# Two SBUF stacks, expert 0's W1 split inside attention, and a reordered last routing quarter

## The chip, the cores and the metric

One core of one Trainium2 chip runs the whole program. The metric is the device time of one execution in microseconds (us); less is better. PE is TensorE, DVE VectorE, ACT ScalarE, POOL GpSimd, and SP the queue of SyncE, which issues transfers.

## The reference: what is computed

The reference chains three layers, all in float32. Clustered attention: queries and keys are given to the nearest of 16 centroids, and a query sees only the keys of its cluster. A mixture of 8 experts: each token goes to its best expert (at most 384 tokens per expert, in token order), weighted by the softmax of the gate. A gated layer (SwiGLU) over all tokens.

```python
mask = q_assign[:, :, :, None] == k_assign[:, :, None, :]
attn = softmax(where(mask, scale * q @ k.T, -1e9))         # 2 batches, 8 heads, 768 x 768
x = (attn @ v) laid out as 1536 tokens x 512
logits = x @ w_gate; e = argmax(logits); gate_w = softmax(logits)[e]
y = relu(x @ w1[e]) @ w2[e]        # tokens of expert e, 512 -> 1024 -> 512
x = gate_w * y
out = (silu(x @ w_gate2) * (x @ w_val)) @ w_out            # 512 -> 1536 -> 512
```

## The kernel before

Attention (`Attention`, lines 24 to 534) works through 16 heads in 8 pairs. A head has 6 tiles of 128 queries, so its loop `run` (L430) has 96 steps g, called slots here. A slot writes out, by the token order in `CFG["order"]`, what each engine does: the exponential of the next tile's scores (token S, `soft`, ACT, L352), every third slot the evacuation of a finished product (E, `evac`, ACT L398 and DVE L400), the scores two tiles ahead (Q, `qk`, PE L339, with the row maximum nm on DVE, L342), the transposes of the tile's probabilities P in two halves (T0 and T1, `pt`, PE L368; ACT copies the first half to SBUF in L371, DVE the second in L373), background work (B0, B1: preparing the next pair), `onat` (O) and every third slot the product with V (V0, `pv`, L387). Each half of the transposes takes a PSUM tile with the tag t from a pool of two buffers (`ps_t`). The scores use two buffers s. Every engine executes its own list in order.

`onat` (L404) turns a finished half of a pair's output into token rows x and adds its part of the gate's logits lg: a matmul with the matrix R (identity and gate weights), and two DVE products with the reciprocal row sums rs (L421).

When the last pair of a batch has a half done, that quarter of the tokens is routed by the generator `Router.route` (L613). It gives control back after every operation, and `trickle` in `run` takes one step of it per slot (token B1), from slot 84 on two (tokens T0 and S). It sums the logits over heads (rlo), takes the maximum, the one-hot roh of the first best expert, the gate weight rgw = 1 / (sum of exponentials + 1e-9), ranks (four small matmuls into another tile t of `ps_t`, L650 to L653, read by DVE in L654), slots in the expert's list (rslot), and then scales each of three tiles of x by rgw (ACT, L666) and scatters it to rows in DRAM (`scatter`, POOL, L602, after a memset of one word named gap). In this generator the rank matmuls and their reader L654 are emitted in the same step.

Behind the loop `run` (L521 to L534) issues the last product, finishes the third quarter's generator, some transposes of the identity that keep PE busy (`warm`), `evac`, `onat`, and the fourth quarter's generator to its end. Then the experts start (`Experts.run`, L936): the read xr of expert 0's rows waits for all scatters, POOL clears Y, four chunks of W1 are split into a high part (ACT cast, L813) and a low part (DVE subtraction, L814), PE runs fillers (L949, L952, L960), DVE computes the offsets of the experts (offi), and expert 0's rows are transposed (`xt`, L841) and split into X, on which the first expert matmul (L879) waits. W2's chunks are split on ACT and POOL inside the expert. `NRAW` = 4 raw buffers hold chunks on their way from DRAM; splitting a chunk issues the read of the one four places on.

All SBUF pools of attention (`at1` to `at3`, and x and lg) are closed together when attention ends; W1, W2 and Y are allocated in their place after that.

Of the kernel before, what the change touches and what calls it, by code (L numbers as in the profile page):

```python
# [23 lines left out]
class Attention:  # L24


    def __init__(self, tc, ctx, q, k, v, cent, gate, x, lg, ident, raw):
# [7 lines left out]
        self.x, self.lg, self.ident, self.raw = x, lg, ident, raw  # L35
        H, S, D, C, E, J = self.H, self.S, self.D, self.C, self.E, self.J
        self.NP = self.B * H // 2
        one = ctx.enter_context(tc.tile_pool(name="at1", bufs=1))
        self.p2 = ctx.enter_context(tc.tile_pool(name="at2", bufs=2))
        self.p3 = ctx.enter_context(tc.tile_pool(name="at3", bufs=3))  # L40
        self.one = one
        self.ps_s = ctx.enter_context(tc.tile_pool(name="ps_s", bufs=2, space=PSUM))
# [3 lines left out]
        self.qB = [one.tile([128, 2, S], F32R, name=f"qB{i}") for i in range(2)]  # L46
        self.kB = [one.tile([128, 2, S], F32R, name=f"kB{i}") for i in range(2)]
        self.R = one.tile([128, H // 2, 2 * D + 2 * E], F32, name="R")
# [21 lines left out]
    def centroids(self):  # L70
# [3 lines left out]
        sq = one.tile([H * C, D], F32, tag="ol", name="sq")  # L74
# [35 lines left out]
    def load(self, n, names="qkv"):  # L110
# [3 lines left out]
        for nm in names:  # L114
            src = getattr(self, nm)
            shape = [128, 2, self.J, self.D] if nm == "v" else [128, self.J, 2, self.D]
            t = self.p2.tile(shape, F32, tag="ld" + nm, name="ld" + nm)
# [15 lines left out]
    def parts(self, n, nm):  # L133
# [5 lines left out]
        st["A" + nm] = self.p2.tile([128, 2, self.S], F32R, tag="A" + nm, name="A" + nm)  # L139
# [182 lines left out]
    def qk(self, g):  # L322
# [4 lines left out]
        if i == 0:  # L327
            if r == 0:
                st["sum"] = self.p3.tile([128, self.J, 2], F32, name="sum")
                st["O"] = self.p2.tile([128, self.S], F32, name="O")  # L330
            self.heads[hd] = dict(P={}, S={}, T={})
# [9 lines left out]
        nm = self.p3.tile([128, 1], F32, name="nm")  # L341
# [3 lines left out]
    def soft(self, g):  # L345
# [5 lines left out]
        P = self.p3.tile([128, 2, HS], F32, name="P")  # L351
# [3 lines left out]
    def pt(self, g, a):  # L355
# [6 lines left out]
        if c == 0 and a == 0:  # L362
            hs["T"][G] = self.p2.tile([128, J, HJ * 128], F32, tag="PT", name="PT")
# [26 lines left out]
    def evac(self, G):  # L390
# [6 lines left out]
        ol = self.one.tile([D, HS], F32, tag="ol", name="ol")  # L397
# [6 lines left out]
    def onat(self, n, half):  # L404
# [6 lines left out]
        rs = self.p2.tile([128, HJ, 2], F32, name="rs")  # L411
# [3 lines left out]
        for jj in range(HJ):  # L415
            j = half * HJ + jj
            nc.tensor.matmul(ps[:, jj, :], lhsT=st["O"][:, j * 128:(j + 1) * 128], rhs=self.R[:, hp, :],
                             start=True, stop=True)
        for dst, c, w in ((self.lg[:, b, js, 2 * hp:2 * hp + 2, :], 2 * D, E),
                          (self.x[:, b, js, 2 * hp * D:2 * (hp + 1) * D].rearrange("p j (r d) -> p j r d", r=2), 0, D)):  # L420
# [9 lines left out]
    def run(self, cent, gate, early, fill, after):  # L430
# [39 lines left out]
        for e in range(self.E):  # L470
            bg.setdefault(14 + 4 * e, []).append(lambda e=e: fill(e))
        self.qk(0)
# [47 lines left out]
        G, n = 2 * NH - 1, self.NP - 1  # L520
        self.pv(G)  # L521
        for _, r in chains:
            while next(r) is not None:
                pass
            moves.append(r)
        self.warm(self.ps_s, "s", 14)
        self.evac(G)
        for _ in self.onat(n, 1):
            pass
        for r in moves:  # L530
            for _ in r:
                pass
        for _ in after(n, 1, lambda: self.warm(self.ps_s, "s", 16)):
            pass  # L534
# [5 lines left out]
class Router:  # L540


    def __init__(self, tc, const, x, lg, cap):
# [11 lines left out]
        self.esl = const.tile([128, J // 2, E], F32, name="esl")  # L555
        self.tok = const.tile([128, B * J], F32, name="tok")
        self.dump = const.tile([128, B * J], F32, name="dump")
        self.cnt = const.tile([128, E], F32, name="cnt")
# [584 lines left out]
NRAW = 4  # L1143
# [99 lines left out]
```

## Time and profile before

| | us |
|---|---|
| runs (3) | 772.0, 772.21, 776.75; median 772.21 |
| the profiled execution | 772.64 |
| its span, first to last instruction | 770.9 |
| PE busy in the span | 748.9 (97%) |
| DVE busy | 518.1 (67%) |
| ACT busy | 396.6 (51%) |
| POOL busy | 267.9 (35%) |

The span holds attention (to about 267 us), the passage to the experts (to 288.71 us), the experts (to about 467 us) and the gated layer. "Busy" of PE counts the fillers too. A timeline row gives the start, the duration, the engine, the line, and the tile written and read; in brackets stands how long the engine had been idle before and whose signal ended that.

### The profile page before, as it was taken

The numbers are of one execution on the slowest core, as the hardware profiler recorded it, in microseconds if no ns is written. First come the engines' busy times: TensorE is split into PE (matmuls) and PEld (weight loads), VectorE is DVE, ScalarE is ACT, GpSimd is POOL, SyncE is SP. The second block draws the span as 40 slices with busy tenths as digits, with TensorE's granted clock in tenths as the row PEclk, the third lists the DMA queues.
The fourth block names the chain that finished last, engine by engine and source line by source line (L and its number), as shares of the span: only waits on it lengthen the run. The fifth ranks groups of instructions, "written<-read, shape, count | busy, mean of one in ns | idle before, by whom it ended". The sixth has DMA issues, their size and how long they took to land.

```text
span 770.9 us, 12615 instructions
## 1 busy us (share of the span) xinstructions
PE 748.9 (97%) x4311; PEld 625.8 (81%) x4311; DVE 518.1 (67%) x875; ACT 396.6 (51%) x738; POOL 267.9 (35%) x244
## 2 busy tenths in 40 slices
PE   8999999999999989999999999999999999999996
PEld 7777777777776679989999998788888888888885
DVE  5668778778787754767676645776766766767433
ACT  5777686777786635667666633454222232222110
POOL 6120210211220177444494432444223333233244
PEclk9899999999999999999999999999999999999999
DMA  8837758537343146787877642232112121110012
GB/s 202 215 76 208 199 185 247 122 84 185 69 131 116 43 165 205 253 247 249 262 242 254 207 127 76 89 102 90 56 58 78 55 82 55 56 55 0 1 55 109
DMA packets 93339, 102.35 MB, mean 133 GB/s; under 512 B 30304, under 2 KB 77408, under 8 KB 93248
## 3 DMA queue, kind: packets, MB, share of 16 engines
q1 hardware_dynamic: 88384, 89.33, 40.4%
q0 software_dynamic: 1920, 6.29, 2.1%
q10 hardware_dynamic: 2944, 5.54, 2.1%
q8 instruction: 55, 0.90, 0.5%
q14 instruction: 36, 0.29, 0.1%
HBM read 68.21 MB, written 12.58 MB: 105 GB/s over the span
## 4 chain that ended last, share of the span: by engine, by line
PE 50%; DVE 4%; ACT 4%; issue 3%; DMA 2%; POOL 1%; ACTq 0%; DVEq 0%; SPq 0%; POOLq 0%
PE o L1104 12%; PE v L1084 11%; PE g L1084 11%; PE yp L879 3%; PE hp L879 3%; PE hp L871 2%; PE yp L871 2%; DMA xr<-moe_rows 2%; PE yp L880 2%; PE hp L880 1%; ACT W1h L813 1%; PE xp L841 1%; ACT W2h L813 1%; DVE cb L1062 1%; POOL out L1115 1%
## 5 line engine op out<-in xcount | busy, mean ns | idle before, releaser
L814 POOL TENSOR_TENSOR W2l<-raw,W2h 128x1024 fp32r<-128x1024 f32 x32 | 76.3, 2401 | 73.7 <-ACT W2h L813 64.8
L342 DVE TENSOR_REDUCE nm<-s 128x1 f32<-128x768 f32 x96 | 91.1, 949 | 12.7 <-PE s L339 11.7
L352 ACT ACTIVATE P<-s,nm 128x768 f32<-128x768 f32 x96 | 86.5, 901 | 13.6 <-DVE nm L342 10.7
L368 PE MATMUL t<-ident,P 128*128 128x128 f32 x576 | 81.8, 275 | 0.8 <-ACT PT L371 0.6
L1093 POOL TENSOR_TENSOR ghl<-u,ghh 128x512 fp32r<-128x512 f32 x36 | 50.0, 1388 | 75.4 <-ACT ghh L1092 75.4
L368 PEld LDWEIGHTS t<-ident,P 128*128 128x128 f32 x576 | 69.1, 141 | 7.8 <-DVE PT L373 2.3
L387 PE MATMUL acc<-PT,ldv 128*64 128x384 f32 x384 | 69.7, 495 | 0.0
L879 PE MATMUL yp<-H,W2h 128*128 128x416 f32 (+1 forms) x224 | 65.3, 363 | 1.7 <-DVE hp L893 1.3
L879 PE MATMUL hp<-X,W1h 128*128 128x416 f32 (+1 forms) x224 | 66.2, 366 | 0.2 <-DVE X L848 0.2
L339 PE MATMUL s<-Ak,Aq 128*128 128x384 f32 x192 | 59.6, 392 | 2.7 <-ACT P L352 2.6
L1112 DVE TENSOR_TENSOR acc<-o,acc 128x512 f32<-128x512 f32 x60 | 41.2, 691 | 30.6 <-PE o L1104 30.6
L371 ACT COPY PT<-t 128x384 f32<-128x384 f32 x96 | 45.7, 476 | 30.1 <-PE t L368 29.9
L1090 DVE TENSOR_TENSOR u<-sg,g 128x512 f32<-128x512 f32 x36 | 24.7, 687 | 54.1 <-ACT sg L1089 54.1
L814 DVE TENSOR_TENSOR W1l<-raw,W1h 128x1024 fp32r<-128x1024 f32 x32 | 49.1, 1562 | 14.7 <-ACT W1h L813 14.4
L1092 ACT CAST ghh<-u 128x512 fp32r<-128x512 f32 x36 | 22.4, 622 | 68.0 <-DVE u L1091 68.0
L880 PE MATMUL hp<-X,W1l 128*128 128x208 f32 (+1 forms) x224 | 56.5, 252 | 0.0
L880 PE MATMUL yp<-H,W2l 128*128 128x208 f32 (+1 forms) x224 | 56.0, 250 | 0.0
L373 DVE COPY PT<-t 128x384 f32<-128x384 f32 x96 | 52.3, 545 | 1.2 <-PE t L368 1.2
L339 PE MATMUL s<-kB,qB 80*128 80x384 f32 (+1 forms) x192 | 51.2, 347 | 1.0 <-ACT kB L274 0.7
L339 PEld LDWEIGHTS s<-Ak,Aq 128*128 128x128 f32 x192 | 29.6, 193 | 27.5 <-ACT P L352 20.1
L387 PEld LDWEIGHTS acc<-PT,ldv 128*64 128x64 f32 x384 | 24.9, 136 | 28.8 <-issue 27.9
L1062 DVE SCALAR_TENSOR_TENSOR cb<-raw,cb 128x512 uint32<-128x512 uint32 x36 | 45.4, 1260 | 1.2
(251 smaller groups left out, 1873.5 us busy)
## 6 DMA issues: line engine op xcount, KB each, us to landing
raw<-in_moe_w SPq DMA_DIRECT2D x64, 512.0 KB, 4.7
Ak<-Hk SPq DMA_DIRECT2D x32, 192.0 KB, 3.9
moe_rows<-zero SPq DMA_DIRECT2D x8, 768.0 KB, 5.1
raw<-in_moe_w_gate SPq DMA_DIRECT2D x12, 512.0 KB, 3.5
raw<-in_moe_w_val SPq DMA_DIRECT2D x12, 512.0 KB, 3.5
raw<-in_moe_w_out SPq DMA_DIRECT2D x12, 512.0 KB, 3.6
xr<-moe_rows ACTq DMA_DIRECT2D x7, 768.0 KB, 6.8
ldq<-in_q SPq DMA_DIRECT2D x16, 192.0 KB, 3.6
```

What stands on the lines that cost most here:

```text
L339: nc.tensor.matmul(ps[:, c, 0:HS], lhsT=ql[:, qs], rhs=kr[:, c * HS:(c + 1) * HS], start=a == 0, stop=a == 1)
L342: nc.vector.tensor_reduce(out=nm, in_=ps[:, :, 0:HS], axis=AX.XY, op=ALU.max, negate=True)
L352: nc.scalar.activation(out=P, in_=ps[:, :, 0:HS], func=AF.Exp, bias=nm, accum_out=self.pairs[n]["sum"][:, i, r:r + 1])
L368: nc.tensor.transpose(ps[:, jj, :], P[:, a, jj * 128:(jj + 1) * 128], self.ident)
L373: nc.vector.tensor_copy(PT[:, js, cs], ps)
L387: nc.tensor.matmul(acc[c * D:(c + 1) * D], lhsT=v[:, c * HJ + j], rhs=PT[:, c * HJ + j, :], start=j == 0, stop=j == HJ - 1, tile_position= ...
L814: (nc.vector if i < 4 else nc.gpsimd).tensor_tensor(out=l, in0=t, in1=h.bitcast(F32), op=ALU.subtract)
L879: self.nc.tensor.matmul(out[:, :, 0:w], lhsT=W[0][:, k, cols], rhs=mov[:, :, k, 0:w], start=k == 0, stop=False)
L880: self.nc.tensor.matmul(out[:, 0, 0:w], lhsT=W[1][:, k, cols], rhs=mov[:, 0, k, 0:w], start=False, stop=k == ks - 1)
L1062: v.scalar_tensor_tensor(out=b, in0=Hw, scalar=0xC0000000, in1=b, op0=ALU.bitwise_and, op1=ALU.bitwise_or)
L1084: nc.tensor.matmul(p, lhsT=W[a], rhs=self.Y[b][:, k, ts], start=i == 0, stop=i == 3 * self.KD - 1)
L1104: nc.tensor.matmul(p[t], lhsT=h[a][:, fc, t * 128:(t + 1) * 128], rhs=W[b][:, fc], start=fc == 0 and i == 0, stop=fc == 1 and i == 2)
```

## The change

1. The pools. Attention's SBUF pools stand on two stacks: on the left what only the preparation of pairs needs, on the right, by lifetime, what the scores, then the products and routing need. Three pools `keep` outlive attention. x is four tiles instead of one, lg lies in one tile with the last of them, and the experts' and the last layer's temporaries use the same tiles of `keep`. The left stack is closed in slot 81, and W1 takes its place.
2. Expert 0's W1. In slot 81 the four raw reads are issued. In slots 85 to 92 each slot splits half a chunk (`piece`): an ACT cast of 128 x 512 and a POOL subtraction. Each second one issues the read of a W2 chunk. Behind attention the four casts and DVE subtractions of W1 are gone; the first two W2 chunks are split there, on ACT and DVE, after a memset of gap that follows the last scatter on POOL, and the clearing of Y comes later.
3. The routing. The exponentials are three ACT operations that sum on the way (`accum_out`), and ACT adds 1e-9. One operation (`scalar_tensor_tensor`) makes the first-best mask from the difference. `edump` folds the subtraction of `dump` into one product. DVE has 4 operations fewer per quarter. The rank matmuls come before the operations et and gw, with the running sum last, and their reader after a pause (`yield True`).
4. The end of `run`. The third quarter's ranks, slots and first scatter are issued before `evac`; the fourth quarter's x is scaled by rs on ACT in six pieces of 128 x 64, and DVE goes from the logits straight to their sum. `warm` has 10 transposes instead of 14, the last filler 14 instead of 24, and the read of expert 0's rows is cut into 1 + 2 tiles instead of 2 + 1.

```diff
-    def onat(self, n, half):
+    def onat(self, n, half, act=None):
...
+            if act and w == D:
+                for jj in range(HJ):
+                    for r in range(2):
+                        act.activation(out=x[:, jj, r], in_=ps[:, jj, r * D:(r + 1) * D], func=AF.Copy,
+                                       scale=rs[:, jj, r:r + 1])
+                yield True
+                return
...
         self.pv(G)
-        for _, r in chains:
-            while next(r) is not None:
-                pass
-            moves.append(r)
-        self.warm(self.ps_s, "s", 14)
-        self.evac(G)
-        for _ in self.onat(n, 1):
-            pass
-        for r in moves:
-            for _ in r:
-                pass
-        for _ in after(n, 1, lambda: self.warm(self.ps_s, "s", 16)):
-            pass
+        on = self.onat(n, 1, nc.scalar)
+        for q, k in ((on, 2), (r, 9)):
+            for _ in range(k):
+                next(q)
+        self.warm(self.ps_s, "s", 10)
+        self.evac(G)
+        for _ in r:
+            pass
+        next(on)
+        last = after(n, 1, lambda: self.warm(self.ps_s, "s", 16))
+        next(last)
+        for q in (on, last):
+            for _ in q:
                 pass
```

Ahead of that `self.pv(G)` the third quarter's generator is now run up to its pause:

```diff
+        while next(r) is not True:
+            pass
         self.pv(G)
```

In `route`:

```diff
-        yield v.tensor_tensor(out=t, in0=lo, in1=bc(mx), op=ALU.is_equal)
-        yield v.tensor_tensor(out=t, in0=t, in1=self.desc, op=ALU.mult)
+        yield v.tensor_tensor(out=d, in0=lo, in1=bc(mx), op=ALU.subtract)
+        for j in range(J):
+            nc.scalar.activation(out=lo[:, j], in_=d[:, j], func=AF.Exp, accum_out=se[:, j:j + 1])
+        nc.scalar.activation(out=se, in_=se, func=AF.Identity, bias=self.eps)
+        yield v.scalar_tensor_tensor(out=t, in0=d, scalar=0.0, in1=self.desc, op0=ALU.is_equal, op1=ALU.mult)
         yield v.tensor_reduce(out=m2, in_=t, axis=AX.X, op=ALU.max)
         yield v.tensor_tensor(out=oh, in0=t, in1=bc(m2), op=ALU.is_equal)
-        yield v.tensor_tensor(out=d, in0=lo, in1=bc(mx), op=ALU.subtract)
-        nc.scalar.activation(out=d, in_=d, func=AF.Exp)
-        yield v.tensor_tensor(out=t, in0=oh.bitcast(F32), in1=self.esl, op=ALU.mult)
-        yield v.tensor_reduce(out=et, in_=t, axis=AX.X, op=ALU.add)
-        yield v.tensor_tensor(out=et, in0=et, in1=self.dump[:, us], op=ALU.subtract)
-        yield v.tensor_reduce(out=se, in_=d, axis=AX.X, op=ALU.add)
-        yield v.tensor_scalar(out=se, in0=se, scalar1=1e-9, scalar2=None, op0=ALU.add)
-        yield v.reciprocal(out=gw, in_=se)
...
+        nc.tensor.matmul(flat(pp), lhsT=self.all, rhs=flat(self.sum), start=False, stop=True)
+        yield v.tensor_tensor(out=t, in0=oh.bitcast(F32), in1=self.edump[:, us], op=ALU.mult)
+        yield v.tensor_reduce(out=et, in_=t, axis=AX.X, op=ALU.add)
+        yield v.reciprocal(out=gw, in_=se)
+        yield True
         yield v.tensor_tensor(out=t, in0=pp, in1=oh.bitcast(F32), op=ALU.mult)
```

In `Experts` and the outermost function:

```diff
+    def piece(self, i, k):
...
+        self.nc.scalar.copy(out=h[:, ks], in_=t[:, ks])
+        self.nc.gpsimd.tensor_tensor(out=l[:, ks], in0=t[:, ks], in1=h[:, ks].bitcast(F32), op=ALU.subtract)
+        if k == 1:
+            del self.loads[0, i]
+            self.load(i + NRAW)
...
-        for i in range(4):
-            self.split(0, i)
+        gap = nc.gpsimd.memset(rt.gap, 0.0)
...
+        for i in range(4, 6):
+            rt.after(self.split(0, i, nc.vector), [gap])
...
+                def first():
+                    at.stages[0].close()
+                    ex.weights(c2, 0)
+                    for i in range(NRAW):
+                        ex.load(i)
+                g0 = 2 * J * (at.NP - 2) + 9
+                spare = {g0: [first]}
+                for i in range(NRAW):
+                    for h in range(2):
+                        spare[g0 + 4 + 2 * i + h] = [lambda i=i, h=h: ex.piece(i, h)]
```

Two places show how the instructions move. In both, the bracket names the engines or transfers whose signals an instruction waits for (DMAHW a transfer, Pool POOL); asp are the scores of the cluster assignment, roh the one-hot, "before", all and sum the matrices of the ranks, on the output of `onat`.

First, PE in slots 61 to 63, while the first quarter is routed. Before:

```order
L202 MATMUL asp<-Xk,cbd 32x384
L339 MATMUL s<-Ak,Aq 128x384 [waits Activation_49]
L339 MATMUL s<-Ak,Aq 128x384
L339 MATMUL s<-kB_90,qB_88 128x384 x2
L368 MATMUL t<-ident,P 128x128 [waits Activation_49]
L368 MATMUL t<-ident,P 128x128 x2
L368 MATMUL t<-ident,P 128x128 [waits DVE_49]
L368 MATMUL t<-ident,P 128x128 x2
L417 MATMUL on<-R,O 128x144 x3
```

And the same place of the changed program:

```order
L212 MATMUL asp<-Xk,cbd 32x384
L669 MATMUL t<-roh,before 128x24 [waits DVE_49,Activation_49]
L671 MATMUL t<-roh,all 128x16
L671 MATMUL t<-roh,all 128x8
L672 MATMUL t<-sum,all 128x24
L349 MATMUL s<-Ak,Aq 128x384 x2
L349 MATMUL s<-kB_110,qB_108 128x384 x2
L378 MATMUL t<-ident,P 128x128 [waits DVE_49]
L378 MATMUL t<-ident,P 128x128 x2
L378 MATMUL t<-ident,P 128x128 [waits Activation_49]
L378 MATMUL t<-ident,P 128x128 x2
L427 MATMUL on<-R,O 128x144 x3
```

The rank matmuls, which stood seven slots later, have come here, and the two transpose halves behind them wait for the other engine than before: the first for DVE, the second for ACT. Slots 63 to 65 and, for the second quarter, 80 to 83 read like this one.

Second, ACT from the last slots to the first exponentials of the fourth quarter. Before (rd is the difference to the maximum, ol half of the last product, rgw the gate weight):

```order
L352 ACTIVATE P,sum<-s,nm 128x768 [waits DVE_49,Activation_49]
L398 COPY ol<-acc 64x384 [waits PE_49,Activation_49]
L371 COPY PT<-t 128x3x128 [waits PE_49] x2
L638 ACTIVATE rd<-rd 128x24 [waits DVE_49]
L398 COPY ol<-acc 64x384 [waits PE_49,Activation_49]
L666 ACTIVATE x<-x,rgw 128x512 [waits DVE_49]
L666 ACTIVATE x<-x,rgw 128x512 x2
L638 ACTIVATE rd<-rd 128x24 [waits DVE_49]
L666 ACTIVATE x<-x,rgw 128x512 [waits DVE_49]
```

And of the changed program (tmp holds the fourth quarter's x, rse the sum of exponentials):

```order
L381 COPY PT<-t 128x3x128 [waits PE_49]
L660 ACTIVATE rlo,rse<-rd 128x8 [waits DVE_49]
L660 ACTIVATE rlo,rse<-rd 128x8 x2
L661 ACTIVATE rse<-rse,eps 128x3 [waits Activation_49]
L381 COPY PT<-t 128x3x128 [waits PE_49]
L686 ACTIVATE x_97<-x_97,rgw 128x512 [waits DVE_49]
L408 COPY ol<-acc 64x384 [waits PE_49]
L686 ACTIVATE x_97<-x_97,rgw 128x512 x2
L435 ACTIVATE tmp<-on,rs 128x64 [waits DVE_49]
L435 ACTIVATE tmp<-on,rs 128x64 x5
L660 ACTIVATE rlo,rse<-rd 128x8 [waits DVE_49]
L660 ACTIVATE rlo,rse<-rd 128x8 x2
```

The third quarter's exponentials stand ahead of the last PT copy instead of behind it, and six scalings of x stand ahead of the fourth quarter's exponentials.

## Rows read from the trace of the kernel before

**Rows 1.** The chain in order of time, 225 to 290: start, us, what.

```profile
278.44 3.76 DMA moe_rows<-x,rslot
...
282.82 3.83 DMA xr<-moe_rows
...
288.71 0.69 PE hp L879
```

**Rows 2.** Timeline behind the loop, and the scatters' line: minimum, median, maximum ns.

```profile
264.59 2.87 PE L387 MATMUL acc<-PT,ldv 128*64 128x384 f32 x12
269.36 0.55 DVE L400 TENSOR_TENSOR O<-acc,ol 64x384 f32<-64x384 f32 x1
271.00 0.21 DVE L421 TENSOR_TENSOR lg<-on,rs 128x48 f32<-128x48 f32 x1 [0.67 <-PE on L417]
271.59 0.50 DVE L631 TENSOR_REDUCE rlo<-lg 128x24 f32<-128x192 f32 x1
272.99 0.18 DVE L636 TENSOR_TENSOR roh<-rt,rm 128x24 fp32r<-128x24 f32 x1
274.12 0.18 DVE L644 RECIPROCAL rgw<-rse 128x3 f32<-128x3 f32 x1
275.00 0.16 DVE L675 TENSOR_TENSOR rslot<-rch,dump 128x3 int32<-128x3 f32 x1
275.91 0.96 POOL L602 DMA_INDIRECT moe_rows<-x,rslot  x1 [2.55 <-ACT x L666]
277.25 4.63 DVE L814 TENSOR_TENSOR W1l<-raw,W1h 128x1024 fp32r<-128x1024 f32 x4 [1.77 <-ACT W1h L813]
278.44 2.01 POOL L602 DMA_INDIRECT moe_rows<-x,rslot  x1 [0.23 <-ACT W1h L813]
...
L602 POOL DMA_INDIRECT moe_rows<-x,rslot x12: 956/958/2007, 220.2 to 278.4; - x12
```

**Rows 3.** Windows: stretch, us, busy (count) of PE, weight loads, DVE, ACT, POOL; clock, DMA, GB/s.

```profile
225.00:264.60 39.60, 38.01 (x248) 27.80 (x246) 29.91 (x74) 27.75 (x59) 3.13 (x6) 1.00 0.27 85
...
285.00:290.00 5.00, 3.57 (x17) 2.88 (x17) 1.18 (x2) 1.01 (x2) 5.00 (x4) 0.73 0.93 299
```

**Rows 4.** Timeline, slot 61: both transpose halves, and ACT's copy of the first.

```profile
178.37 0.82 PE L368 MATMUL t<-ident,P 128*128 128x128 f32 x6
...
178.90 0.48 ACT L371 COPY PT<-t 128x384 f32<-128x384 f32 x1 [0.69 <-PE t L368]
```

**Rows 5.** Timeline, slot 86: the second quarter's rank matmuls between the two halves.

```profile
241.30 0.49 PE L368 MATMUL t<-ident,P 128*128 128x128 f32 x3
241.95 0.28 PE L650 MATMUL t<-sum,all 128*128 128x24 f32 x1 [0.16 <-DVE PT L373]
242.87 0.55 PE L368 MATMUL t<-ident,P 128*128 128x128 f32 x3 [0.31 <-ACT PT L371]
...
241.46 0.90 ACT L352 ACTIVATE P<-s,nm 128x768 f32<-128x768 f32 x1 [0.50 <-DVE rse L643]
242.35 0.47 ACT L371 COPY PT<-t 128x384 f32<-128x384 f32 x1
```

**Rows 6.** Groups of instructions: busy us, mean ns of one, idle time ahead.

```profile
L371 ACT COPY PT<-t 128x384 f32<-128x384 f32 x96 | 45.7, 476 | 30.1 <-PE t L368 29.9
...
L813 ACT CAST W1h<-raw 128x1024 fp32r<-128x1024 f32 x4 | 3.9, 1047 | 0.0
...
L666 ACT ACTIVATE x<-x,rgw 128x512 f32<-128x512 f32 x9 | 6.4, 728 | 0.0
L352 ACT ACTIVATION_READ_ACCUMULATOR P<-s,nm 128x1 f32 x30 | 5.9, 197 | 0.0
...
L638 ACT ACTIVATE rd<-rd 128x24 f32<-128x24 f32 x2 | 0.4, 223 | 4.3 <-DVE rd L637 4.3
```

**Rows 7.** Timeline, slot 68: the first quarter's rank matmuls.

```profile
197.20 0.28 PE L651 MATMUL t<-roh,before 128*128 128x24 f32 x1 [0.63 <-ACT PT L371]
```

**Rows 8.** Timeline, slot 59: the exponential behind the cast of Hq.

```profile
172.50 0.90 ACT L352 ACTIVATE P<-s,nm 128x768 f32<-128x768 f32 x1
```

More of the change, by code (lines that the diff above doesn't have):

```diff
@@ L24, with __init__ @@
 class Attention:
-    def __init__(self, tc, ctx, q, k, v, cent, gate, x, lg, ident, raw):
+    def __init__(self, tc, ctx, q, k, v, cent, gate, keep, ident, raw):
         self.tc, self.nc = tc, tc.nc
@@ L428, in warm, with run @@
             self.nc.tensor.transpose(w[:, 0, :], self.ident, self.ident)
-    def run(self, cent, gate, early, fill, after):
+    def run(self, cent, gate, early, fill, after, spare):
         nc = self.nc
@@ L471, in run @@
             bg.setdefault(14 + 4 * e, []).append(lambda e=e: fill(e))
+        for g, st in spare.items():
+            bg.setdefault(g, []).extend(st)
         self.qk(0)
@@ L661, in route @@
             yield
[L662 to L666 removed]
+            x = self.x[u][:, j]
+            nc.scalar.activation(out=x, in_=x, func=AF.Copy, scale=gw[:, j:j + 1])
             self.scatter(self.slot[:, u * J + j:u * J + j + 1], x)
@@ L940, in run @@
         assert WIDE == rt.CP
-        self.rows(0, nc.sync)
-        for k in range(self.KD):
-            for t in self.Y:
-                nc.gpsimd.memset(t[:, k].bitcast(F32), 0.0)
-        for i in range(4):
-            self.split(0, i)
+        self.rows(0)
+        gap = nc.gpsimd.memset(rt.gap, 0.0)
         w = self.bank("hp")[:, 0]
@@ L1159, in tile_clustered_attention_moe_swiglu @@
         ident = const.tile([128, 128], F32, name="ident")
-        with ExitStack() as c1:
-            xp = c1.enter_context(tc.tile_pool(name="xp", bufs=1))
-            lg = xp.tile([128, B, J, H, E], F32, name="lg")
-            x = xp.tile([128, B, J, DM], F32, name="x")
-            at = Attention(tc, c1, q, k, v, cent, gate, x, lg, ident, raw)
-            at.load0(cent)
-            make_identity(nc, ident)
-            rt = Router(tc, const, x, lg, cap)
-            def after(n, half, idle=None):
-                b, hp = divmod(n, H // 2)
-                return rt.route(2 * b + half, at.p2, at.ps_t, idle) if hp == H // 2 - 1 else None
-            at.run(cent, gate, rt.setup, rt.fill, after)
@@ L1174, in tile_clustered_attention_moe_swiglu, with after @@
-        with ExitStack() as c2:
-            big = c2.enter_context(tc.tile_pool(name="big", bufs=1, reuse_waits="tile"))
-            Y = [big.tile([128, DM // 128, N + 256], F32R, name="Y" + c) for c in "hl"]
-            W1 = [big.tile([128, DM // 128, F], F32R, name="W1" + c) for c in "hl"]
-            W2 = [big.tile([128, F // 128, DM], F32R, name="W2" + c) for c in "hl"]
-            sets = [[w.rearrange("p k f -> p (k f)") for w in W] for W in (W1, W2)]
-            glu = Glu(tc, rt, wg, wv, wo, raw, sets, Y, out)
-            glu.open(c2, True)
+        with ExitStack() as c2:
+            keep = {n: c2.enter_context(tc.tile_pool(name=f"keep{n}", bufs=n, side="right")) for n in (1, 2, 3)}
+            with ExitStack() as c1:
+                at = Attention(tc, c1, q, k, v, cent, gate, keep, ident, raw)
+                at.load0(cent)
+                make_identity(nc, ident)
+                rt = Router(tc, const, at.x, at.lg, cap)
+                ex = Experts(tc, rt, w1, w2, ident, raw, keep)
+                def after(n, half, idle=None):
+                    b, hp = divmod(n, H // 2)
+                    return rt.route(2 * b + half, keep[2], at.ps_t, idle) if hp == H // 2 - 1 else None
+                def first():
[8 more added lines that the diff above has]
+                        spare[g0 + 4 + 2 * i + h] = [lambda i=i, h=h: ex.piece(i, h)]
+                at.run(cent, gate, rt.setup, rt.fill, after, spare)
+            at.stages[1].close()
+            ex.weights(c2, 1)
+            at.stages[2].close()
+            ex.outputs(c2)
+            glu = Glu(tc, ex, wg, wv, wo, out)
+            ex.next = glu.load
```

195 lines of the change are left out of this document (100 added, 95 removed).

## The prediction, made before the change was timed

> **What bounds the kernel now.** I read the page's chain first, then the chain in order of time around the passage from attention to the experts, then the timeline of every engine there, and last the timeline inside the attention loop. In the page's chain most of the time is PE's, on the matmul lines of the last stage and of the experts: from the first matmul of expert 0 to the end, PE is followed by PE. So nothing that the change does to the side engines there can count for much, and the question is when expert 0 starts.
>
> The chain in order of time [rows 1] shows what decides that: the last scatter of routed tokens (278.44, landed 3.76 us later), the read of expert 0's rows (282.82, 3.83 us), transposes, the two splits of X, and the first expert matmul at 288.71. All else near it (the W1 splits, the offsets, the warming matmuls) runs beside. Followed backwards [rows 2], the scatter waits for the chain on VectorE: the last product of probabilities and values ends at 264.59 + 2.87 = 267.46, ScalarE copies half of it, but VectorE adds the halves (O) only at 269.36, since the third quarter's seven routing operations stand ahead; then PE's product `on`, the logits (271.00), the scaling of x, the logits' sum (271.59), the one-hot (272.99), the gate weight (274.12), the slots (275.00, done 275.16), and 0.75 us later the first of three scatters (275.91). They go 1.27 us apart (278.44 less 275.91, halved), and the third takes 2.01 us, the longest of twelve whose median is 0.96.
>
> In the loop ahead, PE is the bound with little to spare: in 225.00 to 264.60 it is busy 38.01 of 39.60 us [rows 3], so a PE wait that is added there is mostly paid in full. Each of the 96 steps (slots) has two halves of three transposes through the two PSUM buffers t, one emptied by ScalarE, the other by VectorE. When both are free the six take about 0.8 us (178.37) [rows 4]. Rows 5 show what happens when one of the two is held: the second quarter's rank matmuls take a buffer between the halves, and the second half starts at 242.87, 1.08 us after the first half's end (241.30 + 0.49), because ScalarE's copy (242.35, 0.47) stood behind an exponential (241.46, 0.90).
>
> **Part 1, the rank matmuls' buffer.** Before, the rank matmuls and VectorE's product that reads them are emitted in one step of the routing generator. Now the matmuls are emitted in the step after the one-hot, and the reader four steps later (the expert's slot base, its sum, the reciprocal and the pause stand between). In the first two quarters a generator step is one slot. So in slots 62 to 65 and again in 80 to 83 one of the two buffers t is held by four finished rank matmuls, and both transpose halves go through the other: the order of the changed program has the first half wait for VectorE and the second for ScalarE there, where they wait the other way round, a whole slot apart, before. PE executes in order, so in each of the eight slots it stands between the halves. With ScalarE free that costs the copy's 0.48 us [rows 6] and its two hand-overs: 0.10 ahead (178.90 less the first half's end, half of 0.82 after 178.37) and 0.05 behind (242.82 to 242.87), 0.63 in all [rows 4, 5]. With an exponential ahead it is rows 5's 1.08. Eight slots are 5.0 to 8.6 us; I take 0.65 each, 5.2, as the slower slots leave ScalarE time to finish its exponential first. PE's idle time of today is swallowed: 1.59 us in the 17 slots of rows 3's first line, about half of it rows 5's own, so 0.05 a slot, 0.4 in eight: 4.8. What goes: PE's wait for the first quarter's ranks (0.63 at 197.20 [rows 7]) and, of rows 5's 1.08, what the four rank matmuls don't fill, some 0.5, with the 0.16 ahead of them: 1.3. Net +3.5. Below, the waits could be hidden altogether, which only idle time of PE could do; the loss of the old stalls would then be left, -1.3. Above, 8.6 - 1.3 = +7.3.
>
> **Part 2, W1 of expert 0 split in slots 85 to 92.** Removed behind attention: four casts on ScalarE (1.05 each) and four subtractions on VectorE (4.63 together) [rows 2, 6]. They lay beside the chain, so by themselves they give nothing; what they did to the scatter is in part 4. Added: eight casts of half the size on ScalarE (at half of 1.05 some 0.55 each, 4.4 in all) and eight subtractions on GpSimd, which is all but idle there (3.13 of 39.60 busy [rows 3]) and on which only scatters queue, none of them urgent yet. ScalarE is busy 27.75 of 39.60 us, so it has room on average. But the next exponential stands behind each cast, and in slots 87 to 89 the second quarter's three scalings of x (0.73 [rows 6]), which came three slots later, now follow the casts directly. Over those three slots ScalarE has three exponentials, their accumulator reads, four copies, three casts and three scalings, by their rows 2.7 + 0.6 + 1.9 + 1.7 + 2.2 = 9.1 us against PE's 7 us for three slots (39.60 x 3 / 17); its rows overlap by about 0.1 each. I take +1.2 for all eight slots. Ends: 0 (all in gaps) and 4.4 (all exposed). The reads of W1 into the raw buffers move nothing: they were issued in the same stretch before, behind the same moves of the last pair, since nothing held them; the four reads of W2 that follow are earlier.
>
> **Part 3, three exponentials with a sum instead of one, per quarter.** One ScalarE operation of 0.22 us becomes three, each with an accumulator read of 0.20 [rows 6], and the addition of 1e-9: 0.42 x 3 + 0.22, some 1.2 us more. In slot 58 they stand between the cast of Hq and an exponential that starts with no idle time behind it (172.50 [rows 8]); the s buffer that it frees is what PE asks for next: +0.7 there. In the second quarter's slot 76 they take the place of an x scaling (0.73) that moves, +0.2. Sum +0.9; ends 0 and 2.2. VectorE's fewer routing operations (0.17 each) lie beside PE: nothing.
>
> **Part 4, the tail.** (a) VectorE runs the third quarter's ranks and slots during the last product, so O follows the copy: 269.36 becomes about 268.1, 1.3 gained. But the third quarter's exponentials (1.5 with reads and addition, some 0.85 of it in idle time) now stand ahead of the last slot's PT copy, and the product, which follows that copy, ends perhaps 0.45 later: 0.85 is left. (b) The scaling of x leaves VectorE: the logits' sum starts 0.4 earlier (271.59 against lg's end at 271.21). One-hot ends at 273.17 - 1.25 = 271.92. (c) From there to the gate weight took 1.13 on VectorE; now the weight waits for ScalarE, which does six scalings of 128x64 out of PSUM from 270.11 on, three exponentials and the addition. No row shows 128x64; the nearest are 0.22 (128x24) and 0.48 (128x384) [rows 6], so six are 1.3 to 2.9 us; by the first row, the nearer, 1.5. Then 1.05 for the exponentials (overlapped) and 0.25: the weight is done at 273.1 instead of 274.30, 1.15 gained, with ends 1.35 and -0.25. (d) The third scatter's 2.01 us: it is the only one that lies wholly inside VectorE's large subtractions (277.25 to 281.88) [rows 2]. Those are gone or held behind the memset of gap, which waits for it: 1.05 gained. Reading the rows of expert 0 as 1 + 2 tiles instead of 2 + 1 leaves the end of the second read where it was. PE's filler, ten transposes shorter, still ends ahead of the read, so the dip of the granted clock to 0.73 of full speed (2.4 GHz) in 285 to 290 [rows 3], behind the idle time of PE ahead of it, stays too. Tail -2.2; ends -3.0 (nothing lost at the PT copy) and +0.25.
>
> The Trainium skill speaks against (d): "SBUF — State Buffer", Who interferes with whom, says that a VectorE operation with two SBUF inputs contends with GpSimd's reads only, and that writing a DMA's descriptors is not among them. By that the 2.01 has another cause, and the sum would be 1.05 us higher. The second scatter, which began about when the subtractions did (1.27 before 278.44) and was not the longest, leans the rule's way; the third stands against it. Of (c), "ScalarE: Activation LUTs", What ACT_TABLE_LOAD costs, gives about 280 ns plus 0.833 ns per element for an operation with a per-partition operand; an estimate by it is 0.33 for each scaling, and the tail would be 0.5 longer.
>
> **The sum** on the profiled execution (772.64; its span is 770.9 and 1.74 lie around it): 3.5 + 1.2 + 0.9 - 2.2 = +3.4, 776.0. The median of the runs is 0.43 lower, so I forecast 775.6.
>
> **Rivals.** R1: the buffer's waits are hidden (PE's waits move, but ScalarE's or VectorE's pace sets the slot anyway) and ScalarE's additions fall into gaps; then the tail and the vanished stalls are left: 772.2 - 2.2 - 1.3 = 768.7. For it: VectorE is busy 29.91 of 39.60 [rows 3], so PE is not alone. Against it: PE's 38.01. R2, slower by over 1%: ScalarE becomes the bound. If in each held slot its copy stands behind an exponential as in rows 5 (1.08 each) and the casts are exposed too, the terms are 8.6 - 1.7 + 3.0 + 1.5 - 2.0 = +9.4: 781.6. It decides from about 0.9 us of waiting per held slot. For it: rows 5 are the only held slot that the trace has. Against it: there the slots were at full pace. R3, the change does not do what it says: the scatter's 2.01 stays by the rule above and ScalarE's six scalings are as slow as 128x384, so that the tail gains nothing, while attention pays its 5.6: 777.8.
>
> **How the numbers follow.** Forecast 0.50, R1 0.22, R2 0.15, R3 0.13. The likeliest is 775.6; its own range is 773 to 778. To leave out no more than 2 in 10 the range takes in R1's time and R3 and stops short of R2's: 768.5 to 781. One per cent, about what a measurement of this kernel can tell from no change, is 7.7 us. Faster by that (below 764.5) needs more than R1 has: 0.04. Slower (above 779.9) is R2: 0.15. Within it: 0.81.
>
> **What would show it.** Right: in slots 62 to 65 and 80 to 83 the two transpose halves stand apart by 0.6 us or more, the second released by ScalarE's PT copy; attention (the last product's end) comes 4 to 6 us later than 267.46; from there to the first expert matmul it takes some 19.5 instead of 21.25 us; all scatters take about 0.96. Wrong: the halves still touch, or the last product ends no later than before (R1); slots 85 to 92 or the held ones stretch by over 1 us each, PE released by ScalarE's exponentials (R2); a last scatter of 2 us (R3).

## The result, and the profile after

The changed kernel takes 780.63 us (median of 7 runs, 779.61 to 783.17) against 772.21 before: ratio 1.0093, 95% interval 1.0068 to 1.0118. The forecast was 775.6. The direction holds, and the stated range, 768.5 to 781, holds by 0.4 us; but its ends had been drawn wide for the rivals, and the forecast's own range, 773 to 778, is missed: 8.4 us came where 3.4 were worked out. By the ratio, which goes by all seven executions of each kernel (three of before's took 774.4 to 776.8), it is 7.2 us, with an interval that lies about the 1% that the prediction drew as its line. The profiled execution took 779.61, with a span of 777.9, which is 7.0 above before's.

Where the 7.0 lie is read from the times at which the same work starts in both traces. (Exponentials are numbered 0 to 95 in order; the expectations below call them by slots.)

| stretch | before | changed | added |
|---|---|---|---|
| exponential 59 | 168.96 | 169.04 | +0.08 |
| exponential 59 to exponential 95 | 92.38 | 99.31 | +6.93 |
| exponential 95 to the last product's end | 6.12 | 6.04 | -0.08 |
| the last product's end to the first expert matmul | 21.25 | 18.43 | -2.82 |
| first to second expert's first matmul (288.71 to 310.83; 292.82 to 313.75) | 22.12 | 20.93 | -1.19 |
| from there to the second run of g products of the last stage (473.87; 477.93) | 163.04 | 164.18 | +1.14 |
| from there to the last two o products (753.56; 760.47) | 279.69 | 282.54 | +2.85 |

**Attention.** The list of PE's waits in 177 to 203; the same line, with the same numbers, stands for 226 to 243. Its columns: us in total, times, longest.

```profile
PE t L378 <- ACT PT L381: 2.3, 4, 0.6
```

Four waits in each of the two windows, on ScalarE's copy of PT: the eight held slots. One of them in the timeline (PE, then ScalarE's copy):

```profile
184.94 0.49 PE L378 MATMUL t<-ident,P 128*128 128x128 f32 x3
186.00 0.55 PE L378 MATMUL t<-ident,P 128*128 128x128 f32 x3 [0.57 <-ACT PT L381]
...
185.47 0.48 ACT L381 COPY PT<-t 128x384 f32<-128x384 f32 x1 [1.16 <-PE t L378]
```

ScalarE had been idle for 1.16 us ahead of that copy, so it is not the bound: it waits for PE, and PE for it, over one buffer. Against [rows 4], where six transposes stand in one row of 0.82, the two halves now reach from 184.94 to 186.55, 1.61 us: 0.79 more in a slot.

**The tail**, in the chain in order of time (start, us, what):

```profile
276.58 0.22 DVE tmp L439
276.82 1.33 ACT tmp L435 x6
278.15 0.57 ACT rlo L660 x6
278.75 0.31 ACT rse L661
279.08 0.19 DVE rgw L675
279.29 1.95 ACT tmp L686 x3
...
282.19 0.94 POOL moe_rows L627
...
283.43 2.71 DMA moe_rows<-tmp,rslot
...
286.87 3.83 DMA xr<-moe_rows
290.70 0.04 issue
290.74 1.44 PE xp L892 x11
```

The logits follow the product's end (274.39) after 2.19 instead of 3.54 us [rows 2]. The six scalings take 1.33, and the gate weight waits for ScalarE as foreseen. All three last scatters take 0.96, the third ends 10.0 us behind the product instead of 13.0, and the read of expert 0's rows leaves 2.9 us sooner.

**The clock behind it** (columns as in [rows 3]):

```profile
285.00:290.00 5.00, 3.69 (x16) 2.60 (x15) 1.87 (x2) 0.00 (x0) 5.00 (x4) 1.00 0.63 198
290.00:295.00 5.00, 3.60 (x25) 3.33 (x26) 1.18 (x2) 1.01 (x2) 5.00 (x4) 1.00 0.90 249
```

The granted clock stays at 1.00 of 2.4 GHz where before's row had 0.73. The first eight matmuls of expert 0 take 1.32 us instead of 2.21 (288.71 to 290.92; 292.82 to 294.14); that is 0.9 of the 1.19. The rest is most likely the two W2 chunks that are now split ahead of the experts. Before, the cast of one stood on ScalarE ahead of H, the first expert's hidden values, and a matmul of PE came late. The shifted kernel before (an experiment below), which is the program before up to the last stage, had no dip of the clock and took 21.60 us in this stretch, 0.67 more than the changed kernel's 20.93:

```profile
290.72 1.05 ACT L813 CAST W2h<-raw 128x1024 fp32r<-128x1024 f32 x1
291.67 0.52 ACT L899 ACTIVATE H<-hp 128x416 fp32r<-128x416 f32 x1
...
293.18 0.44 PE L879 MATMUL hp<-X,W1h 128*128 128x416 f32 x1 [0.50 <-PE hp L880]
```

No step of the prediction had this term.

**The last stage.** Groups by operation; the first fence is the kernel before, the second the changed one (busy us, mean ns of one, idle time ahead):

```profile
L1104 PE MATMUL o<-W2h,ghh 128*128 128x512 f32 x72 | 28.0, 389 | 0.0
L1084 PE MATMUL g<-Yh,W2h 128*128 128x512 f32 x72 | 28.0, 389 | 0.0
```

```profile
L1165 PE MATMUL o<-W2h,ghh 128*128 128x512 f32 x72 | 28.5, 396 | 0.0
L1145 PE MATMUL g<-Yh,W2h 128*128 128x512 f32 x72 | 28.1, 390 | 0.0
```

The same matmul, with no wait ahead of it, is 7 ns longer in o and in a few of the g's that follow. In the timeline of the changed kernel o's matmuls start 0.2340 us apart on the average where nothing is waited for, before's 0.2267; g and v differ little. It is 24 matmuls of an o and some six behind them, 0.2 us, and fifteen o's, the second to the sixteenth of eighteen, make the 2.85 (with 0.17 less ahead of the first). No step of the prediction spoke of this stage.

### The profile page after: what moved, and what is told of

Read it like the earlier page. It is cut to its first block, busy times and chain, and to the rows that moved or that the text cites. A ratio compares the mean times of both kernels' runs of the same rounds, so it can differ in the third digit from the quotient of the medians.

```text
span 777.9 us, 12611 instructions
## 1 busy us (share of the span) xinstructions
PE 751.8 (97%) x4298; PEld 624.7 (80%) x4298; DVE 513.7 (66%) x856; ACT 400.9 (52%) x772; POOL 272.1 (35%) x251
## 4 chain that ended last, share of the span: by engine, by line
PE 77%; DVE 7%; ACT 7%; DMA 3%; issue 3%; POOL 1%; ACTq 0%; DVEq 0%; SPq 0%; POOLq 0%
PE o L1165 12%; PE g L1145 11%; PE v L1145 11%; PE acc L397 8%; PE s L349 8%; PE t L378 7%; PE yp L930 3%; PE hp L930 3%; PE hp L922 2%; PE yp L922 2%; ACT P L362 2%; DMA raw<-in_moe_w 2%; PE yp L931 2%; PE hp L931 2%; DMA xr<-moe_rows 1%
## 5 line engine op out<-in xcount | busy, mean ns | idle before, releaser
L853 POOL TENSOR_TENSOR W2l<-raw,W2h 128x1024 fp32r<-128x1024 f32 x30 | 71.5, 2401 | 79.9 <-ACT W2h L852 79.8
L378 PE MATMUL t<-ident,P 128*128 128x128 f32 x576 | 83.6, 276 | 5.8 <-ACT PT L381 5.1
L853 DVE TENSOR_TENSOR W1l<-raw,W1h 128x1024 fp32r<-128x1024 f32 x28 | 44.3, 1602 | 13.2 <-ACT W1h L852 12.8
L410 DVE TENSOR_TENSOR O<-acc,ol 64x384 f32<-64x384 f32 x32 | 17.6, 550 | 45.7 <-ACT ol L408 45.7
```

What stands on the lines that cost most here:

```text
L378: nc.tensor.transpose(ps[:, jj, :], P[:, a, jj * 128:(jj + 1) * 128], self.ident)
L853: j = (low or (nc.vector if i < 4 else nc.gpsimd)).tensor_tensor(out=l, in0=t, in1=h.bitcast(F32), op=ALU.subtract)
```

## The experiments

Theory A: the held buffer is what attention lost. Theory C: o is slow by where its operands lie in SBUF. Rival B: ScalarE became the bound. All ratios are to the kernel before, in rounds on the same chip. Differences to the changed kernel's median are between separate rounds, in which the median of the kernel before was 772.2 to 773.5; the sizes below rest on the traces.

**Ranks next to their reader.**

```diff
-        pp = <rank matmuls>           # behind the one-hot
+        if u >= 2: pp = <rank matmuls>
...
         yield True
+        if u < 2: pp = <rank matmuls>
         yield v.tensor_tensor(out=t, in0=pp, in1=oh.bitcast(F32), op=ALU.mult)
```

> The changed kernel, with the rank matmuls of the first two quarters emitted in the same generator step as VectorE's product that reads them; nothing else differs. Theory A (the held PSUM buffer): in the changed kernel the exponentials of slots 63 to 69 fall back by 3.8 us against before and those of slots 79 to 88 by 3.5 us, because both transpose halves go through one buffer; with the buffer held for one step only, both go, some 0.5 of each as a single wait stays, and the end of the last product of probabilities and values comes at about 268 to 269 instead of 274.4; the whole time falls by 5 to 7 us. Rival B (ScalarE sets the slot there: the three exponentials with their reads, the casts and the x scalings): the slots stretch as much with the buffer free, and the time falls by less than 2 us.

Measured: 775.42 us, ratio 1.0037 (1.0023 to 1.0051); 5.2 us below the changed kernel's median. PE's list of waits in 177 to 200 has one line left, and none on PT:

```profile
PE s L349 <- ACT P L362: 0.3, 1, 0.3
```

How far the exponentials stand behind before's, less the offset at number 59 (the start of an execution differs from before's by up to 2.3 us), in this run and in two that follow:

| exponential | changed | late ranks | late ranks and one exponential | no pieces |
|---|---|---|---|---|
| 60 | 0.89 | 0.90 | 0.09 | 0.89 |
| 69 | 4.66 | 1.28 | 0.48 | 4.67 |
| 79 | 3.83 | 0.49 | -0.59 | 3.86 |
| 88 | 7.37 | 2.00 | 1.14 | 7.11 |
| 95 | 6.93 | 1.59 | 0.44 | 6.08 |

A stands: the buffer costs 6.93 - 1.59 = 5.3 us by number 95. B falls.

**ghh and ghl moved by 32 bytes, in the changed kernel and in the one before.** One line in the last stage's pool, behind u in the first and ahead of gh in the second:

```diff
+        if g == 0 and tb == 0 and fc == 0:
+            nc.gpsimd.memset(self.p2.tile([128, 8], F32, name="pad", bufs=1), 0.0)
```

> The changed kernel, with one more buffer of 32 bytes per partition in the last stage's pool of two buffers, behind the others, so that the tiles ghh and ghl (the stationary operands of the output product o) begin 32 bytes lower, at an address that leaves 32 and not 0 on division by 64, as they did before the change; one small memset is added on GpSimd. Theory C (address): the matmuls of o, spaced 0.2335 us in the changed kernel and 0.2267 before, go back to 0.2267, and with them the six matmuls behind each o; 18 times 0.2 us, the time falls by 3.0 to 3.6 us. Rival D (something else in that stage, such as the engines' traffic beside PE or the clock): the spacing stays at 0.2335 and the time stays within 0.5 us of the changed kernel's.

> The kernel before, with the same 32 bytes ahead of ghh and ghl in the last stage's pool, so that they begin at an address that leaves 0 on division by 64, as in the changed kernel. Theory C (address): o's matmuls are spaced 0.2335 us instead of 0.2267 from the second o on, and the time rises by 3.0 to 3.6 us. Rival D: no change within 0.5 us. A third way: if it is the place of o's operands relative to each other and not that of ghh and ghl, the one shift works and the other doesn't.

Measured: 782.2 us, ratio 1.0104 (1.0076 to 1.0131), o at 0.2334: nothing gained. And 775.24, ratio 1.0033 (1.0023 to 1.0042) for the shifted kernel before, o at 0.2332:

```profile
L1106 PE MATMUL o<-W2h,ghl 128*128 128x512 f32 x72 | 28.5, 396 | 0.0
```

So the place decides, but not by the rest on division by 64. The third way of the second expectation is what came: the one shift works, the other doesn't. By the tile addresses of the built programs, on division by 128, W1, W2 and Y leave 96 in both kernels, ghh and ghl 96 before, 64 in the changed kernel, 32 and 0 in these two runs. Only the equal pair was fast.

**No pieces of W1 in attention.**

```diff
-        for i in range(NRAW):
-            for h in range(2):
-                spare[g0 + 4 + 2 * i + h] = [lambda i=i, h=h: ex.piece(i, h)]
...
         gap = nc.gpsimd.memset(rt.gap, 0.0)
+        for i in range(4):
+            self.split(0, i)
```

> The changed kernel, with W1 of expert 0 split behind attention as before the change (four casts of 128x1024 on ScalarE and four subtractions on VectorE), nothing of it in slots 85 to 92. Theory A: these slots cost little (the exponentials are 7.0 us behind before's in slot 86 and 7.0 in slot 95), so the last product ends 0 to 1.2 us earlier; behind attention ScalarE's casts stand ahead of nothing on the chain. Of the scatters: if VectorE's subtractions are what made the last scatter last 2.01 us before, the scatter that lies inside them takes 2.0 us again and expert 0 starts 1.05 us later than it would otherwise; if not, all take 0.96. Rival B (ScalarE is the bound in slots 85 to 92): the last product ends 2 to 4 us earlier. Sum: within 1.5 us of the changed kernel by A, 2 to 4 us less by B.

Measured: 787.0 us, ratio 1.0185 (1.0168 to 1.0202): both theories missed the time. In attention A's number came, 6.93 - 6.08 = 0.85 us less (table). Behind it, this edit makes a wait of its own. The queue SP, then the chain in order of time:

```profile
284.35 0.82 SPq L876 DMA_DIRECT2D xr<-moe_rows  x2
285.28 10.32 SPq L843 DMA_DIRECT2D raw<-in_moe_w  x6
```

```profile
285.79 7.10 DMA raw<-in_moe_w
292.91 1.05 ACT W2h L852
293.99 0.57 DVE W2l L853
...
295.26 0.46 DVE X L899
```

The reads of the W2 chunks now stand in SP's list behind the read of expert 0's rows, which waits for the last scatter. They start from 285.28 on, the second lands at 292.89, and its split stands ahead of X on VectorE; PE waits until 295.86, and the first expert then takes 23.31 us instead of 20.93, with the granted clock at 0.50 (1.2 GHz) in 295 to 300, behind 5 us without a matmul. In the kernel before, those chunks were split behind X. The run therefore doesn't price the pieces against the tail. It does show the scatter again (POOL, then VectorE):

```profile
279.03 0.96 POOL L627 DMA_INDIRECT moe_rows<-tmp,rslot  x1 [0.22 <-ACT W1h L852]
280.30 1.97 POOL L627 DMA_INDIRECT moe_rows<-tmp,rslot  x1 [0.22 <-issue]
...
279.08 4.63 DVE L853 TENSOR_TENSOR W1l<-raw,W1h 128x1024 fp32r<-128x1024 f32 x4 [1.75 <-ACT W1h L852]
```

**Equal rests.** ghh and ghl at rest 96 (the pad with 24 elements in place of 8), and, in another run, W1, W2 and Y at rest 64, ghh and ghl where the change had put them:

```diff
+        if l == 0:
+            self.nc.gpsimd.memset(pool.tile([128, 24], F32, name="pad"), 0.0)
         setattr(self, nm, [pool.tile([128, k, n], F32R, name=nm + c) for c in "hl"])
```

> The changed kernel, with 96 bytes per partition in place of the 32, so that ghh and ghl begin at an address that leaves 96 on division by 128, as W1, W2 and Y do in both kernels and as ghh and ghl did before (in the changed kernel it is 64, in the first shifted one 32, in the shifted kernel before 0, and o was slow in all three). Theory C2 (o's two operands are read at full pace where their addresses leave the same rest on division by 128): o goes back to 0.2267 us, the time falls by 3.0 to 3.6 us. Rival D: o stays at 0.2335.

> The changed kernel, with 96 bytes ahead of W1 on the left stack, so that W1, W2 and Y move from rest 96 to rest 64 on division by 128, where ghh and ghl lie in the changed kernel; ghh and ghl are not moved. If C2 holds as a relation of the two operands, o goes to 0.2267 us and the products g and v (W against Y, both at 64) stay at 0.2265: 3.0 to 3.6 us less. If the rest of 96 by itself is what is fast, o stays at 0.2335 and g and v, 864 matmuls, become as slow: some 6 us more than the changed kernel.

Measured: 778.66 us, ratio 1.0069 (1.0050 to 1.0088), and 777.36, 1.0046 (1.0030 to 1.0062): 2.0 and 3.3 us below the changed kernel's median. o is at 0.2268 and 0.2269, and g and v at 0.2269 and 0.2268 in the second. Two groups of the second:

```profile
L1167 PE MATMUL o<-W2h,ghl 128*128 128x512 f32 x72 | 28.0, 389 | 0.0
L1147 PE MATMUL v<-Yh,W2h 128*128 128x512 f32 x72 | 28.0, 389 | 0.0
```

It is the relation of the stationary and the moving operand: 389 ns at 96 with 96 and at 64 with 64, 396 at 96 with 64, 32 and 0. That 128 is the number is not shown: the equal pairs leave the same rest on division by 256 and 512 too, so what the runs show is that a difference of 32, 64 or 96 bytes was slow and no difference fast. From the second run of g products to the last two o's both runs take 0.2 us less than before took, against 2.85 more in the changed kernel.

**Both edits, and one exponential.**

```diff
-        for j in range(J):
-            nc.scalar.activation(out=lo[:, j], in_=d[:, j], func=AF.Exp, accum_out=se[:, j:j + 1])
-        nc.scalar.activation(out=se, in_=se, func=AF.Identity, bias=self.eps)
+        if u < 2: nc.scalar.activation(out=lo, in_=d, func=AF.Exp)
+        else: <as above>
...
+        if u < 2:
+            v.tensor_reduce(out=se, in_=lo, axis=AX.X, op=ALU.add)
+            v.tensor_scalar(out=se, in0=se, scalar1=1e-9, scalar2=None, op0=ALU.add)
         yield v.reciprocal(out=gw, in_=se)
```

> The changed kernel with both edits: the rank matmuls in the step of their reader in the first two quarters, and ghh and ghl at rest 96. If the two are independent, as theories A and C2 have it, 5.2 and 3.0 to 3.6 us come off the changed kernel's 780.6: 771.8 to 772.4, the time of the kernel before. If only the first works, 775.4.

> The same with one exponential per quarter again in the first two quarters (VectorE sums and adds 1e-9 there, as before); the last two quarters keep three with a sum. The three exponentials, their reads and the addition stood in slots 58 and 76; the first cost 0.9 us by the fall back of the exponential of slot 60, the second little. Expected 0.9 us less than the run with both edits (0.5 to 1.5), so 771 to 771.5, 1 us below the kernel before; if the fall back of slot 60 is paid back later anyway, no difference.

Measured: 772.32 us, ratio 0.9987 (0.9972 to 1.0002), and 771.27, ratio 0.9977 (0.9961 to 0.9993). The two edits add up. One exponential gives 1.59 - 0.44 = 1.15 us in attention (table; 1.12 against the run with both edits), about the 1.05 between the medians; the intervals overlap, so the trace carries this, not the times. This version is faster than both kernels.

**What stretches a scatter.** The split of W2 not held behind the last scatter, and then VectorE's subtraction replaced by copies, which leaves out the low part of these chunks:

```diff
-            rt.after(self.split(0, i, nc.vector), [gap])
+            self.split(0, i, nc.vector)                       # first run
+            for _ in range(2): nc.vector.tensor_copy(l, h.bitcast(F32))   # second run, in place of the subtraction
```

> The kernel of the run with both edits and one exponential, where the two subtractions of W2 on VectorE (two operands of 128x1024 in SBUF, 1.2 us each) no longer wait for the memset behind the last scatter, so that they run beside the second or third of the last scatters, about 276 to 278.5. Theory E (VectorE's work of two SBUF operands stretches a scatter that lies inside it): the third scatter takes about 2.0 us in place of 0.96, as it did in the kernel before (2.01) and in the run without the pieces (1.97), and expert 0's read and first matmul come some 1 us later than in the run that this one is made from. Rival F (the long scatter has another cause, such as its place as the third): 0.96, and the first matmul is where it was or earlier.

> The same, with each of the two subtractions replaced by two copies of the same size on VectorE (one SBUF operand); the low part of W2's first two chunks is thereby a copy of the high part, the subtraction is left out. Theory E, if it is the second operand that counts: the third scatter takes 0.96 us. If any VectorE work of that size does it: about 2.0 us.

One execution each, 770.25 and 775.71 us. First run, POOL and VectorE:

```profile
276.74 1.40 POOL L627 DMA_INDIRECT moe_rows<-tmp,rslot  x1 [0.22 <-issue]
...
276.09 2.35 DVE L866 TENSOR_TENSOR W2l<-raw,W2h 128x1024 fp32r<-128x1024 f32 x2
```

The third scatter lies inside the subtractions and takes 1.40, 0.44 more than 0.96. From exponential 95 to the first expert matmul this run takes 25.09 us, 0.47 more than the run it is made from (24.62). E's direction holds and F falls; the size is half of that expected. Second run, VectorE's copies (minimum, median, maximum ns), and POOL:

```profile
L1016 DVE CAST W2l<-W2h x4: 694/767/13131, 274.0 to 288.6; 128x1024 fp32r<-128x1024 f32 x4
```

```profile
274.32 0.52 POOL L626 MEMSET gap<- 1x1 f32 x1
274.62 1.03 POOL L627 DMA_INDIRECT moe_rows<-tmp,rslot  x1
...
275.69 1.61 POOL L1020 MEMSET Yh<- 128x1792 f32 x1
...
286.42 1.61 POOL L1020 MEMSET Yl<- 128x1792 f32 x1
```

The scatter takes 1.03, so it is not any VectorE work of that size that stretches it; the memset of gap ahead of it took 0.52 instead of 0.09. It is one copy that suffers: the third of the four, begun at 275.45, took 13.13 us, beside GpSimd's eight memsets, which follow each other to 288.03; the others took 0.84, 0.69 and 0.69.

**One exponential in the third quarter too** (u < 3 in the edit above).

> The kernel of the run with both edits and one exponential, with one exponential in the third quarter too (there they stand on ScalarE ahead of the last slot's copy of PT, on which the last product waits). Expected: the last product ends 0.3 to 0.5 us earlier against the exponential of slot 95, and the time is 0.3 to 0.5 us less; if VectorE's two more operations (0.17 each) stand in the way of the halves' sum instead, no difference.

Measured: 770.31 us, ratio 0.9966 (0.9951 to 0.9981), the lowest of all. But the expected cause isn't there: the last product ends 6.12 us behind exponential 95 (260.31 to 266.43), as before and in the run that it is made from (6.12 each; 6.04 in the changed kernel). The intervals of this run and of the one it is made from overlap; whether there is a gain is open.

## Why the prediction was off by 5 us

- **Part 1, right in mechanism, too small.** Eight waits on ScalarE's copy, as said; the price was 5.3 net against 3.5. The step that failed is "0.65 each": it took the gap between the halves from the end of one to the start of the next. Back to back, matmuls overlap: six take 0.82, two halves alone 0.49 and 0.55 [rows 4, 5]. The held slot loses that overlap too: 0.79. Eight times 0.79, less the 0.4 of idle time and the 1.3 of old stalls that the prediction took off, are 4.6, closer to 5.3. By the table the first quarter's four slots cost 3.3 (number 79) and the second's 2.0, though PE waits 2.3 us in each; the late-ranks run has three waits of PE of its own, 1.0 us together, in the second. Attention ended 6.93 us later than before, where the sign of being right said 4 to 6.
- **Part 2**, 1.2 forecast: removing the pieces gave 0.85, and 0.44 is what is left in attention once buffer and exponentials are put right, with the x scalings in it. Somewhat too high.
- **Part 3**, 0.9: measured 1.15, of which 0.8 at exponential 60, behind the seven small operations that stand ahead of it. Right.
- **Part 4, the tail**: -2.2 was -2.65 from the product's end and +0.45 for a later product. Measured -2.82; the later product did not come (6.04 against 6.12). By these terms the passage would take 18.6 us; the 19.5 that the prediction gave as its sign doesn't follow from them, and 18.43 came. Of (c), the six scalings took 1.33 where 1.5 were forecast: each lasts 0.31 to 0.34, but they start 0.20 apart; the sentence that made the tail 0.5 longer counted them end to end. (d) came as forecast: all scatters 0.96 when VectorE's large subtractions are gone or held. By the Trainium skill's "SBUF — State Buffer", Who interferes with whom, descriptor writing isn't among what these subtractions disturb; four runs here (2.01, 2.02 in the shifted kernel before, 1.97, 1.40) against 0.96 elsewhere and 1.03 beside copies speak against it as far as the whole scatter goes. Which part of the scatter is stretched, the writing of its descriptors or the reading of rslot, is open. So is why the scatter ahead of it never is: in three runs it began 0.05 to 0.08 us before the first subtraction, lay beside it from there on, and took 0.96 (279.03 in the run without the pieces).
- **"The dip ... stays too"** was wrong for this execution. That gave 0.5 to 0.9 back: 0.9 by the first eight matmuls, 0.5 by the shifted kernel before, which had no dip (21.60 against 22.12). But the dip is no property of either kernel. The runs with equal rests are the same program but for addresses, start the transposes of X at 289.44 and 289.55, and in 290 to 295 had a clock of 0.66 in the one and 1.00 in the other. Between the spans' 7.0 and the medians' 8.4 lie 1.4 us: the profiled execution of the kernel before took 0.4 more than its median, the changed one's 1.0 less, the fastest of its seven. Whether the clock made that is not shown.
- **What was left out: the last stage**, 2.85 us, and on the other side the W2 casts that no longer stand in the first expert, some 0.3 to 0.7 us back. The prediction followed the pools' new places only for waits and lifetimes, and took the same instructions to cost the same at other addresses.
- The +1.14 between the second expert and the last stage is not put down to the change: the shifted kernel before, whose program is unchanged up to there, took 1.5 us longer than before in the same stretch; over all runs it took 163.0 to 165.3.

That the time still fell inside the range is luck in part: its ends were drawn for the rivals, the upper one just short of R2's time. R2's time, 781.6, is near the measured one, but its mechanism is not: the held slots waited 0.57, below its 0.9, and ScalarE idled ahead of its copies. R1 and R3 fall by the waits and the scatters.

## What to carry to other kernels

A PSUM buffer taken by a small product counts from its matmul to its reader, in steps of whatever rides in between; emit the matmul next to the reader, or give it its own buffer. When pools move, compare the addresses of the two operands of the matmuls that run back to back, not only whether they fit, and time the pair: the expert products below lost nothing. And price a broken run of matmuls by first start to last end, not by the gap.

## What the runs showed of the hardware that was not expected

Matmuls of 512 columns, each with its weight load, start 0.2267 us apart when stationary and moving operand leave the same rest on division by 128 bytes, and 0.2332 to 0.2340 when not (three unequal pairs, three equal ones, which are equal on division by 512 too). By "TensorE: Matmul & The Clock Gate" of the Trainium skill, What happens when you issue a matmul, loading the next weights takes no read bandwidth from the running matmul. That gives no reason for the 3% here, which hang on the two operands' places; why they do is not shown. The expert products, whose X and H the change also moved to rest 64, show nothing of it: the second expert takes 18.89 us in the changed kernel (313.75 to 332.64) and 18.91 before (310.83 to 329.74).

A copy on VectorE can stand still through a whole row of GpSimd memsets (13.13 us for one that takes 0.69 alone), while subtractions of two operands beside the same memsets were not seen to be stretched: in the changed kernel the two of W2, from 284.52 on beside memsets that run from 284.42 to 296.8, took 2.36 together.
